# Reordering the tokens of a fused attention + MLP kernel: even tokens first, and transposed queries and keys used straight from the DMA

## The chip, the cores and the metric

The kernel runs on one core of one Trainium2 chip. The metric is the device time of one execution in microseconds (us); three executions of the kernel before took 322.33 to 323.25 us, median 322.83. The profile that is read here is of one execution, with a span of 321.3 us between its first and last instruction.

## The reference, cut to what matters

```python
batch, n_heads, seq, head_dim = (8, 8, 576, 64)          # q, k, v, float32
scores = q @ k.T / 8; mask = abs(pos_q - pos_k) <= 32    # a window of 65 keys per query
attn = softmax(where(mask, scores, -1e9)); a = attn @ v
x = a.transpose(0, 2, 1, 3).reshape(4608, 512)           # 4608 tokens x (8 heads x 64)
h = x @ w_in                                             # w_in 512 x 2048
out = maximum(0.01 * h, h) @ w_out                       # w_out 2048 x 512
```

## The kernel before, in words

**Attention** is cut into 64 instances: batch b (8), half hf of the 576 tokens (2 x 288), pair p of heads (4). Instance i has b = i // 8, hf = (i // 4) % 2, p = i % 4. The two heads of a pair lie on partitions 0 to 63 and 64 to 127. Before, pair p holds heads p and p + 4.

What an instance needs is made as follows. `load_qk` (L73) and `load_v` (L82) bring q, k and v in float32 from DRAM, on the queue of SP. `cast_qk` (L183) turns q and k to bf16 on GpSimd (POOL), on 96 partitions with six tokens each. Then they are transposed, so that head dimension lies on the partitions: for batches 0 to 2 by TensorE (L214, six 96x96 transposes into a PSUM tile `tp` and one ScalarE copy, L222 or L228, into token order); for batches 3 to 7 by a DMA transpose (L200) into a tile of its own, and again one ScalarE copy (L222, L228), SBUF to SBUF, which puts the six residues of the token number back in token order. `place_keys` (L240) copies the transposed keys on VectorE (DVE) into `kbd`, a block-diagonal weight (two copies of 64 partitions x 576 per pair). `cast_v` (L191, or L189 on ScalarE) does the same for v, into `vbd`.

`score` (L255) multiplies five blocks of 64 keys with the queries in their windows, 544 columns in all, into one PSUM tile `ps` of which there is one; ScalarE takes the exponential (L261), POOL multiplies with a 0/1 mask (L265) into `prob`. `join` (L276, from instance 12 on) adds the two halves of `prob` on DVE so that `sums` (L285) needs one matmul of 288 columns; DVE takes the reciprocal (L296). `product` (L307, five matmuls) multiplies with `vbd`, and `scaled` (L322) writes x times the reciprocal into `xT`, the transposed input of the MLP. There is one PSUM buffer for the sums and one for the products.

**The MLP** follows in groups of 288 tokens. `h_tile(g, f)` makes 128 of the 2048 hidden values of a group with four matmuls of 288 columns (L336); `h_out` applies the leaky ReLU on ScalarE from PSUM into `gT` (L342). `o_tile(j)` makes 128 output tokens with 16 matmuls of 512 columns (L373), one ScalarE copy (L378) and one store (L379) on SP. The h and o tiles and the TensorE transposes share a PSUM pool of four buffers.

**The order** on each engine is the program's: `manual_schedule()` keeps it. The first part (batch 0, group 0, batch 1's transposes and group 1's h tiles) is written out by hand. After it a plan of h tiles and quarters of o tiles is walked; `spend` holds a clock in planned us and calls `step()` for the next instance whenever its due time is reached, spread so that the last instance of a group comes `LEAD` = 4 us before the group's first h tile. A `step()` for instance i issues the join of i + 1, the score of i + 2, then sums, product and scaling of i, then whatever transposes, key copies, casts and loads are due. A PLAN table and the counters `state["tp"]` and `asked` say which. Weights `w_in` (8 DMAs) and `w_out` (4) are loaded and cast by DMAs that POOL issues (L465, L471).

Of the kernel before, what the change touches and what calls it, by code (L numbers as in the profile page):

```python
# [16 lines left out]
def kernel(  # L17
# [11 lines left out]

    nc = tc.nc  # L30

    B, H, S, D = q.shape
    W = 32
# [9 lines left out]
    NCOL = 544  # L43
# [10 lines left out]
    tdma = ctx.enter_context(tc.tile_pool(name="tdma", bufs=1))  # L54
# [9 lines left out]

    def load_qk(b, p, behind=None):


        for into, src, name in ((qf, q, "qf"), (kf, k, "kf")):
            t = fload.tile([96, 2, RUN * D], FP32, name=f"{name}{p}")
            if behind is not None:  # L70
                behind.memset(t[0:1, 0, 0:1], 0.0)
                behind = None
            nc.sync.dma_start(  # L73
                out=t, in_=src[b, p:H:NPAIR].rearrange("a (p c) d -> p a (c d)", c=RUN),
            )
            into[b, p] = t

    def load_v(b, p):

        t = fload.tile([128, NB, D], FP32, name=f"vf{p}")  # L80
        for a in range(2):
            nc.sync.dma_start(  # L82
                out=t[64 * a:64 * a + 64],
                in_=v[b, NPAIR * a + p].rearrange("(c p) d -> p c d", p=64),
            )
        vf[b, p] = t
# [29 lines left out]
    def clear(t, p):  # L116
# [4 lines left out]

    nc.vector.memset(kbd[0], 0.0)
# [6 lines left out]

    PAD = 32  # L130
    SPLIT = [HALF - PAD, HALF]
    WIN = [
        [(1, 32, 128), (3, 160, 128), (0, 0, 96), (2, 96, 128), (4, 224, 64)],
        [(4, 288, 64), (6, 352, 128), (8, 480, 96), (5, 288, 128), (7, 416, 128)],
    ]

    win = const.tile([128, 3, 128], BF16)
    nc.gpsimd.memset(win, 1.0)
    for lo in (0, 64):
# [3 lines left out]
            base=0, channel_multiplier=-1, pattern=[[0, 3], [1, 128]],  # L143
# [3 lines left out]
            base=2 * W, channel_multiplier=1, pattern=[[0, 3], [-1, 128]],  # L147
        )
    nc.gpsimd.memset(vbd[0][:, 3], 0.0)
    win_f = win.rearrange("p n c -> p (n c)")  # L150
    mask = [const.tile([128, NCOL], BF16, name=f"mask{i}") for i in range(2)]

    def make_masks():
        for hf in range(2):
            lo = (0, 2 * W)[hf]
            nc.gpsimd.tensor_copy(
                out=mask[hf][:, 0:SPLIT[hf]], in_=win_f[:, lo:lo + SPLIT[hf]],
            )
            lo = (W, 0)[hf]
            nc.gpsimd.tensor_copy(  # L160
                out=mask[hf][:, SPLIT[hf]:NCOL], in_=win_f[:, lo:lo + NCOL - SPLIT[hf]],
            )
    NPROB = 6
    prob = const.tile([128, NPROB, NCOL + 2 * PAD], BF16)
    nc.vector.memset(prob[:, :, 0:PAD], 0.0)
    nc.vector.memset(prob[:, :, PAD + NCOL:], 0.0)

# [9 lines left out]
    def cast_qk(b, p, q_eng=None):  # L177
        for eng, src, dst in ((q_eng or nc.gpsimd, qf, qb), (nc.gpsimd, kf, kb)):
            tok = src[b, p].rearrange("p a (c d) -> p c a d", d=D)
            if eng is nc.scalar:  # L180
                eng.activation(out=dst[:, p], in_=tok, func=AF.Copy)
            else:
                eng.tensor_copy(out=dst[:, p], in_=tok)  # L183
# [9 lines left out]

    BY_DMA = 3
    qkT, asked = {}, {}

    def transpose_dma(b, p):
        for which, src in (("q", qb), ("k", kb)):
            t = tdma.tile([128, RUN, 96], BF16, name=f"{which}T{p}")
            nc.sync.dma_start_transpose(out=t, in_=src[:, p].rearrange("p c a d -> p (c a d)"))  # L200
            qkT[b, p, which] = t
        asked[b, p] = state["done"]

    def transposes(b):

        qT[b] = attn.tile([128, NPAIR, S], BF16, name="qT")
        for p in range(NPAIR):
            for which, src in (("q", qb), ("k", kb)):
                if b >= BY_DMA:
                    tp = qkT.pop((b, p, which))  # L210
                else:
                    tp = mmps.tile([128, RUN, 96], BF16, name="tp", tag="mm")
                for c in range(RUN if b < BY_DMA else 0):
# [6 lines left out]
                tok = tp.rearrange("p c i -> p i c")  # L220
                if which == "q":
                    nc.scalar.activation(  # L222
                        out=qT[b][:, p].rearrange("p (i c) -> p i c", c=RUN), in_=tok, func=AF.Copy,
                    )
                else:
                    kT = kt.tile([128, S], BF16, name="kT")
                    kT_v = kT.rearrange("p (i c) -> p i c", c=RUN)
                    nc.scalar.activation(out=kT_v, in_=tok, func=AF.Copy)  # L228
# [3 lines left out]
    unplaced = []  # L232

    def place_keys():

        while unplaced:
            b, p, kT = unplaced.pop(0)
            for a in range(2):
                r = slice(64 * a, 64 * a + 64)
                nc.vector.tensor_copy(  # L240
                    out=kbd[b % 2][r, p, :, r],
                    in_=kT[r].rearrange("p (n j) -> p n j", j=64),
                )
# [6 lines left out]
    def score(i):  # L250
        b, hf, p = where(i)
        ps = scps.tile([128, 1024], FP32, name="ps")
        lo = c0 = 512 - SPLIT[hf]
        for blk, q0, n in WIN[hf]:
            nc.tensor.matmul(  # L255
                ps[:, c0:c0 + n], kbd[b % 2][:, p, blk],
                qT[b][:, p, q0:q0 + n], start=True, stop=True,
            )
            c0 += n
        e = attn.tile([128, NCOL], BF16, name="e")  # L260
        nc.scalar.activation(  # L261
            out=e, in_=ps[:, lo:lo + NCOL], func=AF.Exp, scale=scale,
        )
        pr = prob[:, i % NPROB, PAD:PAD + NCOL]
        nc.gpsimd.tensor_mul(pr, e, mask[hf])  # L265
        probs[i] = [pr, None, None]
        state["ps"] = ps

    def join(i):


        hf = where(i)[1]
        lo = PAD * hf
        t = prob[:, i % NPROB]
        both = joined.tile([128, HALF], BF16, name="both")
        nc.vector.tensor_add(both, t[:, lo:lo + HALF], t[:, lo + HALF:lo + 2 * HALF])  # L276
        probs[i][1] = both

    def sums(i):
# [6 lines left out]
        else:  # L286
            nc.tensor.matmul(
                s, ones_bd, pr[:, (NCOL - HALF) * (1 - hf):(NCOL - HALF) * (1 - hf) + HALF],
                start=True, stop=False, skip_group_check=True,
            )  # L290
            nc.tensor.matmul(
                s[:, PAD * (1 - hf):PAD * (1 - hf) + NCOL - HALF], ones_bd,
                pr[:, HALF * hf:HALF * hf + NCOL - HALF], start=False, stop=True, skip_group_check=True,
            )
# [4 lines left out]
    def product(i):  # L299
# [4 lines left out]
        c0 = 0  # L304
        for n_, (blk, q0, n) in enumerate(WIN[hf]):
            a = q0 - HALF * hf
            nc.tensor.matmul(  # L307
                x[:, a:a + n], vbd[b % 2][:, p, blk, :], pr[:, c0:c0 + n],
                start=(n_ == 0), stop=(n_ == len(WIN[hf]) - 1), skip_group_check=True,
            )  # L310
            c0 += n
# [29 lines left out]
    def h_out(g, f, h):  # L341
        nc.scalar.activation(  # L342
            out=gT[:, f, ds(g * HALF % RING, HALF)], in_=h[:, 0:HALF], func=AF.Prelu, alpha=0.01,
        )
# [36 lines left out]
    def keep_busy(t, lo, n):  # L381


        for _ in range(n):
            nc.tensor.matmul(
                t[:, lo:lo + 224], ones_bd, mask[0][:, 0:224], start=False, stop=False,
# [6 lines left out]
    state = {"tp": 8, "done": 0}  # L393
    t_parts = {}
# [3 lines left out]

    PLAN = (
        ((0, 0, 0, 0, 0, 2, 4, 6), ((), (), (), (), (0,), (1, 2), (3,), ()),  # L400
         ((), (), (), (), (), (), (0,), (1, 2, 3))),
        ((0, 1, 2, 3, 4, 5, 6, 7), ((0,), (1,), (2,), (3,), (), (), (), ()),
         ((), (), (), (), (0,), (1,), (2,), (3,))),
    )

    def step_transposes(upto):
        while state["tp"] < min(upto, 8 * B):
            b = state["tp"] // 8
            if b not in t_parts:
                t_parts[b] = transposes(b)  # L410
            next(t_parts[b])
            state["tp"] += 1

    def step():
# [3 lines left out]
        b, r = i // 8, i % 8  # L418
        if JOINED - 1 <= i < NC - 1:
            join(i + 1)  # L420
        if b < BY_DMA - 1:
            place_keys()
        if b > 0:
            upto = 8 * (b + 1) + (PLAN[b > 1][0][r] if b + 1 < BY_DMA else 0)
            step_transposes(max(upto - 1, 8 * (b + 1)))
        if 8 <= i < NC - 2:
            nb, _, np_ = where(i + 2)
            if nb >= BY_DMA:
                step_transposes(8 * nb + 2 * np_ + 2)
                if any(key[:2] == (nb, np_) for key in unplaced):  # L430
                    place_keys()
# [3 lines left out]
        if b > 0:  # L435
            step_transposes(upto)
        if 0 < b < B - 1:
            for p in PLAN[b > 1][1][r] if b + 1 <= BY_DMA else ():
                cast_qk(b + 1, p)
                if b + 1 == BY_DMA:  # L440
                    transpose_dma(b + 1, p)
                if b + 2 < B:
                    load_qk(b + 2, p)

            n, p = (b + 1, 3) if r == 0 else (b + 2, r - 4)
            if p in range(4 if r == 0 else 3) and BY_DMA < n < B:
                step_transposes(8 * (n - 1) + 2 * p + 2)
                place_keys()
                cast_qk(n, p)
                transpose_dma(n, p)  # L450
                if n + 1 < B:
                    load_qk(n + 1, p)
            for p in PLAN[b > 1][2][r]:
                cast_v(b + 1, p)
                if b + 2 < B:
                    load_v(b + 2, p)
# [3 lines left out]
    w_in_r = moe_w_in.rearrange("(a u d) f -> a d u f", a=2, d=D)  # L460
# [209 lines left out]
```

The softmax here doesn't subtract the row's maximum and nothing guards it: scores larger than these inputs give would overflow.

## Time and profile before

| | busy us | share of 321.3 us | what it does most |
|---|---|---|---|
| PE (TensorE) | 303.9 | 95% | h tiles 134.3, o tiles 128.6 |
| ACT (ScalarE) | 223.6 | 70% | gT 103.4; the 40 SBUF-to-SBUF copies of L222 and L228 47.2 |
| DVE (VectorE) | 212.7 | 66% | reciprocals 125.1; key copies 28.5 |
| POOL (GpSimd) | 182.3 | 57% | masks 77.8; casts of v, k and q 86.8 |
| PEld (weight load) | 205.9 | 64% | overlaps PE |

An engine's busy time is no limit by itself: the table shows which engine has no room, and that a long ScalarE copy need not cost anything if PE never waits for it. The DMA queues moved 48.28 MB; HBM was read for 36.70 MB.

### The profile page before, as it was taken

To read this page: it belongs to the slowest core of one execution; us is meant where nothing else is said; L and a number is where in the kernel's file an instruction comes from. 1 tells how busy PE (TensorE), PEld (TensorE's weight loads), DVE (VectorE), ACT (ScalarE), POOL (GpSimd) and SP (SyncE) were. 2 spreads that over 40 slices of the span, in tenths; PEclk is the share of its full clock that TensorE was granted. 3 is DMA by queue.
4 is the path that set the end of the run, shared out by engine and by line. 5 is a ranking of instruction groups with operands and counts; after the bars stand their busy time and mean duration, and the time that the engine had idled before them with its cause. 6 is when DMAs were issued, how large, how long until landed. Compare 5 with 4: busy or idle time off the path is not lost.

```text
span 321.3 us, 6563 instructions
## 1 busy us (share of the span) xinstructions
PE 303.9 (95%) x2476; PEld 205.9 (64%) x2497; DVE 212.7 (66%) x259; ACT 223.6 (70%) x432; POOL 182.3 (57%) x215
## 2 busy tenths in 40 slices
PE   2779999999999999999999999999999999999995
PEld 1566775586765857676665857676665857576753
DVE  5788784986757679676748778677747666565100
ACT  7586584296658897888887887888885837464631
POOL 8999967677945976269612885269612653230000
PEclk9999999999999999999999999999999999999999
DMA  8999998999997999929991399728611000000101
GB/s 185 229 176 233 267 236 208 259 224 233 207 192 192 214 242 234 175 73 179 236 221 71 94 216 229 177 65 134 166 39 65 36 34 35 33 36 0 67 33 66
DMA packets 85168, 48.28 MB, mean 150 GB/s; under 512 B 64016, under 2 KB 80656, under 8 KB 85136
## 3 DMA queue, kind: packets, MB, share of 16 engines
q1 hardware_dynamic: 80848, 43.66, 62.8%
q0 software_dynamic: 4288, 4.20, 8.0%
q8 instruction: 19, 0.31, 0.4%
q14 instruction: 13, 0.11, 0.2%
HBM read 36.70 MB, written 9.44 MB: 144 GB/s over the span
## 4 chain that ended last, share of the span: by engine, by line
PE 79%; POOL 6%; DMA 6%; DVE 4%; ACT 3%; issue 2%; POOLq 0%; DVEq 0%; ACTq 0%
PE mm L373 35%; PE mm L336 33%; DMA w_out_bf<-in_moe_w_out_dram 6%; PE x L307 4%; PE ps L255 4%; DVE r L296 2%; PE s L285 2%; POOL prob L265 2%; POOL kb L183 1%; ACT kT L228 1%; DVE xT L322 1%; PE tp L214 1%; POOL w_in_bf L465 1%; ACT e L261 1%; ACT gT L342 0%
## 5 line engine op out<-in xcount | busy, mean ns | idle before, releaser
L296 DVE RECIPROCAL r<-s 128x288 f32<-128x288 f32 x64 | 125.1, 1955 | 56.6 <-PE s L285 53.5
L336 PE MATMUL mm<-xT,w_in_bf 128*128 128x288 bf16 x1024 | 134.3, 286 | 0.9 <-DMA w_in_bf<-in_moe_w_in_dram 0.7
L265 POOL TENSOR_TENSOR prob<-e,mask 128x544 bf16<-128x544 bf16 x64 | 77.8, 1215 | 99.6 <-ACT e L261 79.5
L373 PE MATMUL mm<-w_out_bf,gT 128*128 128x512 bf16 (+2 forms) x571 | 128.6, 373 | 1.6 <-DMA w_out_bf<-in_moe_w_out_dram 0.5
L342 ACT ACTIVATE gT<-mm 128x288 bf16<-128x288 f32 x256 | 103.4, 413 | 24.9 <-PE mm L336 10.0
L336 PEld LDWEIGHTS <-w_in_bf 128*128 128x128 bf16 x1024 | 97.8, 98 | 25.6 <-issue 1.8
L373 PEld LDWEIGHTS <-gT 128*128 128x128 bf16 x592 | 56.0, 98 | 59.9 <-issue 0.6
L378 ACT ACTIVATE o_sb<-mm 128x512 f32<-128x512 f32 (+2 forms) x37 | 21.7, 586 | 53.8 <-PE mm L373 53.8
L261 ACT ACTIVATE e<-ps 128x544 bf16<-128x544 f32 x64 | 39.8, 622 | 9.5 <-PE ps L255 8.8
L191 POOL CAST vbd<-vf 64x576 bf16<-64x576 f32 x58 | 38.5, 663 | 3.7 <-DMA vf<-in_v_dram 1.9
L240 DVE COPY kbd<-kT 64x576 bf16<-64x576 bf16 x64 | 28.5, 445 | 16.3 <-ACT kT L228 15.6
L322 DVE TENSOR_TENSOR xT<-x,r 128x288 bf16<-128x288 f32 x64 | 29.3, 458 | 9.0 <-PE x L307 2.4
L183 POOL CAST kb<-kf 96x768 bf16<-96x768 f32 x32 | 28.6, 895 | 2.6 <-DMA kf<-in_k_dram 2.6
L255 PEld LDWEIGHTS <-kbd 128*128 128x128 bf16 x320 | 21.5, 99 | 10.2 <-DVE kbd L240 1.4
L255 PE MATMUL ps<-qT,kbd 128*128 128x128 bf16 (+2 forms) x320 | 26.3, 214 | 1.7 <-DVE kbd L240 1.2
L307 PE MATMUL x<-prob,vbd 128*128 128x128 bf16 (+2 forms) x320 | 26.0, 213 | 1.1 <-DVE xT L322 1.0
L307 PEld LDWEIGHTS <-vbd 128*128 128x128 bf16 x320 | 21.4, 99 | 3.9 <-DVE xT L322 1.0
L222 ACT ACTIVATE qT<-qT 128x576 bf16<-128x576 bf16 x20 | 23.6, 1182 | 0.0
L228 ACT ACTIVATE kT<-kT 128x576 bf16<-128x576 bf16 x20 | 23.6, 1180 | 0.0
L276 DVE TENSOR_TENSOR both<-prob 128x288 bf16<-128x288 bf16 x52 | 22.8, 438 | 0.6
L183 POOL CAST qb<-qf 96x768 bf16<-96x768 f32 x24 | 19.7, 823 | 0.0
L285 PE MATMUL s<-both,ones_bd 128*128 128x288 bf16 x52 | 14.9, 286 | 0.0
(45 smaller groups left out, 102.0 us busy)
## 6 DMA issues: line engine op xcount, KB each, us to landing
qf<-in_q_dram SPq DMA_DIRECT2D x32, 288.0 KB, 4.2
kf<-in_k_dram SPq DMA_DIRECT2D x32, 288.0 KB, 4.6
vf<-in_v_dram SPq DMA_DIRECT2D x64, 144.0 KB, 4.9
out_dram<-o_sb SPq DMA_DIRECT2D x35, 256.0 KB, 2.8
w_in_bf<-in_moe_w_in_dram POOLq DMA_DIRECT2D x8, 256.0 KB, 7.9
w_out_bf<-in_moe_w_out_dram POOLq DMA_DIRECT2D x4, 512.0 KB, 16.3
qT<-qb SPq DMA_TRANSPOSE x20, 4.0
kT<-kb SPq DMA_TRANSPOSE x20, 3.3
```

The costliest lines, as they stand in the source:

```text
L183: eng.tensor_copy(out=dst[:, p], in_=tok)
L191: nc.gpsimd.tensor_copy(out=vbd[b % 2][r, p, :, r], in_=vf[b, p][r])
L240: nc.vector.tensor_copy(out=kbd[b % 2][r, p, :, r], in_=kT[r].rearrange("p (n j) -> p n j", j=64),)
L255: nc.tensor.matmul(ps[:, c0:c0 + n], kbd[b % 2][:, p, blk], qT[b][:, p, q0:q0 + n], start=True, stop=True,)
L261: nc.scalar.activation(out=e, in_=ps[:, lo:lo + NCOL], func=AF.Exp, scale=scale,)
L265: nc.gpsimd.tensor_mul(pr, e, mask[hf])
L296: nc.vector.reciprocal(r, s)
L307: nc.tensor.matmul(x[:, a:a + n], vbd[b % 2][:, p, blk, :], pr[:, c0:c0 + n], start=(n_ == 0), stop=(n_ == len(WIN[hf]) - 1), skip_group_c ...
L322: nc.vector.tensor_mul(place(i), x, r)
L336: nc.tensor.matmul(h[:, 0:HALF], w_in_bf[:, c, ts(f, 128)], xT[:, c, ds(g * HALF % RING, HALF)], start=(c == 0), stop=(c == DMC - 1),)
L342: nc.scalar.activation(out=gT[:, f, ds(g * HALF % RING, HALF)], in_=h[:, 0:HALF], func=AF.Prelu, alpha=0.01,)
L373: nc.tensor.matmul(o[:, lo:hi], gT[:, f, ds(128 * j % RING, 128)], w_out_bf[:, f, lo:hi], start=(f == 0), stop=(f == FFC - 1),)
```

## The change: what it does

- In every half of 288 tokens, the even tokens come first and then the odd ones, from the queries through `prob`, x and `xT` to the h matmuls. `h_out` undoes it: it reads PSUM with the two parities interleaved and writes `gT` in token order.
- For batches 2 to 7 q and k are loaded in rows of two tokens (512 bytes) instead of six (1536 bytes), and cast in two pieces each, so that the DMA transpose delivers the queries in the even-first order. It writes right into `qT` and `kT`; the ScalarE copies that followed it are gone, and batch 2 is no longer transposed by TensorE. The keys' order is undone in the DVE copy into `kbd`, which then writes with a step of two elements. It is issued two steps after the transpose.
- Batches 0 and 1 keep the TensorE transposes and ScalarE copies; only the order in which the copy of the queries reads PSUM differs.
- Score, mask and `prob` have 576 columns (two layers of 288) instead of 544; matmuls of a block run over two stretches (even, odd) and have the same total of 544 columns. `ps` is one fixed tile.
- Pairs are heads 2p and 2p + 1, so `w_in` is loaded in its natural order, by 4 DMAs of 128 partitions instead of 8 of 64. The loads of `w_in` and `w_out` are issued one place earlier.
- v of batch 1 is cast by ScalarE instead of POOL; the due times of instances 8 to 11 move a little, and the second half's instances go behind h tiles 7, 11, 14 instead of 7, 10, 13. q and k of batch b are cast at steps 8(b-1)+2 to +5 and v at +6 to +9, for all b from 2 on, instead of by the PLAN table.

```diff
-    BY_DMA = 3
+    BY_DMA = 2
 load_qk:
-            nc.sync.dma_start(out=t, in_=src[b, p:H:NPAIR].rearrange("a (p c) d -> p a (c d)", c=RUN))
+            heads = src[b, 2 * p:2 * p + 2]
+            if b < BY_DMA:
+                nc.sync.dma_start(out=t, in_=heads.rearrange("a (p c) d -> p a (c d)", c=RUN))
+            else:
+                nc.sync.dma_start(
+                    out=t.rearrange("p a (g e) -> p a g e", g=3),
+                    in_=heads.rearrange("a (g p c) d -> p a g (c d)", g=3, c=2),
+                )
 cast_qk:
+                by_c = src[b, p].rearrange("p a (g c d) -> c p g a d", g=3, c=2)
+                parts = [(dst[:, p, 3 * c:3 * c + 3], by_c[c]) for c in range(2)]
 transpose_dma:
-            t = tdma.tile([128, RUN, 96], BF16, name=f"{which}T{p}")
-            nc.sync.dma_start_transpose(out=t, in_=src[:, p].rearrange("p c a d -> p (c a d)"))
-            qkT[b, p, which] = t
+        for t, src in ((qT[b][:, p], qb), (kT, kb)):
+            nc.sync.dma_start_transpose(
+                out=t.rearrange("p (c i) -> p c i", c=RUN),
+                in_=src[:, p].rearrange("p c a d -> p (c a d)"),
+            )
+        landing.append((state["done"], b, p, kT))
 place_keys:
+        while landing and landing[0][0] + 2 <= state["done"]:
+            unplaced.append(landing.pop(0)[1:])
...
+                    nc.vector.tensor_copy(
+                        out=to.rearrange("p n (m c) -> p n c m", c=2),
+                        in_=kT[r].rearrange("p (c n m) -> p n c m", c=2, n=NB),
+                    )
 score:
-        nc.scalar.activation(out=e, in_=ps[:, lo:lo + NCOL], func=AF.Exp, scale=scale)
-        nc.gpsimd.tensor_mul(pr, e, mask[hf])
+        nc.scalar.activation(out=e, in_=ps[:, P0:P0 + 2 * HALF], func=AF.Exp, scale=scale)
+        nc.gpsimd.tensor_mul(pr.rearrange("p n c i -> p (n c i)"), e, mask[hf].rearrange("p n c i -> p (n c i)"))
 h_out:
-            out=gT[:, f, ds(g * HALF % RING, HALF)], in_=h[:, 0:HALF], func=AF.Prelu, alpha=0.01,
+            out=gT[:, f, ds(g * HALF % RING, HALF)].rearrange("p (i c) -> p i c", c=2),
+            in_=h[:, 0:HALF].rearrange("p (c i) -> p i c", c=2), func=AF.Prelu, alpha=0.01,
 step:
+    for b in range(2, B):
+        for p in range(NPAIR):
+            qk_due.setdefault(8 * (b - 1) + p + 2, []).append((b, p))
+            v_due.setdefault(8 * (b - 1) + p + 6, []).append((b, p))
...
 load_w_in:
-        for a in range(2):
-            nc.gpsimd.dma_start(out=w_in_bf[64 * a:64 * a + 64, :, f0:f1], in_=w_in_r[a, :, :, f0:f1])
+        nc.gpsimd.dma_start(out=w_in_bf[:, :, f0:f1], in_=w_in_r[:, :, f0:f1])
 before and in the plan:
-        prev = 0.9 * O_US * 4 if i < 12 else at[i // 4 - 1] - LEAD
-        due.append(prev + (at[i // 4] - LEAD + (1.2 if i < 12 else 0) - prev) * (i % 4 + 1) / 4)
+        prev = 0.75 * O_US * 4 if i < 12 else at[i // 4 - 1] - LEAD
+        due.append(prev + (at[i // 4] - LEAD + (1.8 if i < 12 else 0) - prev) * (i % 4 + 1) / 4)
-    cast_v(1, 0)
+    cast_v(1, 0, on_act=True)
-                cast_v(1, i - 7)
+                cast_v(1, i - 7, on_act=True)
```

## The prediction, made before the changed kernel was run

> **What bounds the kernel now.** I read the busy times first, then PE in windows, then who waited for whom, then the chain of work that ended last, then the costs of the operations that the change touches. The table of windows shows PE busy 47.57 of the first 60 us, 79.15 of the next 80, 159.42 of the next 160:
>
> ```profile
> 0.00:60.00 60.00, 47.57 (x435) 33.81 (x439) 44.41 (x52) 39.11 (x75) 51.44 (x68) 1.00 1.08 222
> 60.00:140.00 80.00, 79.15 (x662) 53.48 (x667) 58.93 (x77) 60.41 (x116) 50.05 (x58) 1.00 1.04 208
> 140.00:300.00 160.00, 159.42 (x1261) 107.22 (x1270) 109.38 (x132) 115.47 (x223) 80.79 (x90) 1.00 0.49 108
> ```
>
> So from 60 us on TensorE is the bound and hardly waits; what can be won there is TensorE work itself. Only the first 60 us hold idle PE time (12.4 us, of which 5.6 lie before PE's first instruction). The chain says what ends that part:
>
> ```profile
> 29.51 19.63 DMA w_out_bf<-in_moe_w_out_dram
> 49.14 0.04 issue
> 49.18 2.75 PE mm L373 x12
> ```
>
> The last quarter of `w_out` lands at 49.14 us, and the first o tile waits for it. PE waits before that are paid again at this wait, so shortening them wins nothing unless the weights come earlier. The engine queues in the waits view and the rows of the touched operations:
>
> ```profile
> PE x L307 <- DVE xT L322: 1.0, 4, 0.4
> PE mm L373 <- DMA w_out_bf<-in_moe_w_out_dram: 0.5, 1, 0.5
> ...
> L342 ACT ACTIVATE gT<-mm 128x288 bf16<-128x288 f32 x256 | 103.4, 413 | 24.9 <-PE mm L336 10.0
> L222 ACT ACTIVATE qT<-qT 128x576 bf16<-128x576 bf16 x20 | 23.6, 1182 | 0.0
> L222 ACT ACTIVATE qT<-tp 128x576 bf16<-128x576 bf16 x12 | 7.9, 655 | 4.5 <-PE tp L214 4.5
> L240 DVE COPY kbd<-kT x64: 399/448/451, 7.7 to 244.4; 64x576 bf16<-64x576 bf16 x64
> L183 DVE CAST qb<-qf x7: 630/1262/2258, 4.8 to 45.4; 96x768 bf16<-96x768 f32 x7
> ```
>
> The reader is to see: a ScalarE copy that gathers six residues costs 1182 ns out of SBUF and 655 out of PSUM; the key copy takes the same 448 ns always, while the seven DVE casts take 630 to 2258.
>
> [...] For ScalarE the trace agrees on SBUF (1182) and shows no penalty on PSUM (655 for 576 elements, beside 622 for 544 in a row, L261). [...] the new copy itself is in no run here.
>
> **The change part by part**, against the span of 321.3 us. The three timed runs have a median of 322.83, 1.5 above it; I add 1.5 at the end.
>
> 1. Batch 2's TensorE transposes go: eight groups of six, 0.26 us each in the chain ("PE tp L214 x6"), all on PE between 67 and 84 us where it is the bound: **-2.1 us**.
> 2. 40 ScalarE copies go (47.2 us), and 8 from PSUM. ScalarE isn't the bound: its busy share is 70%. On the path they show only around 107 to 121 us, where the chain runs over qT and kT copies, the key copies behind them, and a reciprocal that is late for it; there PE waits for xT at 121.48 (0.28) and 125.88 (0.20). **-0.5**. A third such wait at 58.32 (0.15) should go with the wider due times of instances 8 to 11: **-0.15**.
> 3. Sums of instances 0 to 11: 576 columns instead of 544, 32/2.4 = 13 ns each, **+0.15**. Scores and products keep their columns. That a matmul's operands come in two stretches no row shows: [...] I take 0[...].
> 4. Exponential and mask: 32 columns more, +0.03 and +0.07 us (622/544 and 1215/544 per column). In the middle both are two steps ahead of their use. Before 25 us they are in a dependent chain, but that ends at the weights' wait: 0.
> 5. `h_out` reads PSUM in alternation. Between 413 (no penalty, as `tp` shows) and 413 + 288 x 0.92 = 680 ns (the SBUF surcharge, (1182-655)/576 per element). I take 413: 0.
> 6. Casts of q and k in halves: v's 576 columns take 665 ns and 768 take 820, so about 185 fixed; +0.19 us a cast, 48 casts, +9 us on POOL. It loses batch 1's v casts (8 x 0.665) and four w_in issues. POOL stays under 60%: 0. SP: the 512-byte rows make 576 pieces a load, as v's 64 x 9 have; v's issue takes 0.63 us against 0.44. A step then needs two transposes (2 x 1.22), two loads and a store, 4.2 us of SP in a step of 4.1 to 4.5. Stores wait behind, four output buffers deep: 0 on PE.
> 7. **The key copies as a new wait on DVE.** A step on DVE is now 0.31 (join) + 1.95 + 0.46 + two copies, 3.79 us from 99.98 to 103.77, thus 2.88 + 2k. Queued behind the copies are the next join, reciprocal and scaling; PE's product waits for the scaling before it, with about 1.2 us of slack, over a step of 4.2. At k = 0.53 (the undisturbed cast's 630 ns for 768 elements; scaled to 576 it is 0.47, with part of it fixed 0.53) nothing is lost; at k = 1.06 (waiting for POOL each time, as the median cast does with twice the shortest) the lag grows by 0.8 a step over four steps of six batches. I take k = 0.8, a wait at every second copy: a lag of 0.84 after three steps, still in the slack, and **+0.4** for steps that fall closer together; bounds 0 and +7. The wait for the landing itself: transposes land 3.3 to 4.0 us after issue, the copy comes two steps (8.4 us) after the cast was issued, whose last piece ends some 4.6 us into its step: covered.
> 8. **v of batch 1 on ScalarE.** POOL waits for these data now; its casts start at 48.09 and 49.62, each "<-DMA vf". ScalarE executes in order: behind its two casts stand the copies of pair 2's transposes (done at 45.2 to 46.5 now), the exponential of instance 9 and pair 3's copies; PE's transposes of pair 3 wait for a PSUM buffer of pair 2's, and score 10 for its keys. Casts end at 49.62+0.68 = 50.3, q's and k's copies at 51.6, key copies at 52.5; score 10 runs at 51.77 now: +0.8. If the buffer decides, transposes wait to 50.95 where 49.18 was: +1.8. If v lands earlier, 0. I take **+0.8**.
> 9. Weights: POOL issues four w_in DMAs (0.79 each, as w_out's equal shape) for eight of 0.66. The DMA share is 1.1 to 1.3 from 5 to 50 us, so the queue is full and an earlier issue moves the end little: 0, with -0.5 (PE's wait) as the other end.
>
> Sum: -2.1 - 0.5 - 0.15 + 0.15 + 0.4 + 0.8 = -1.4; 321.3 - 1.4 = 319.9, and with 1.5 **321.4 us**.
>
> **The rivals.** *Nothing is given back* (chance 0.24): v lands with the weights a little earlier and the key copies don't collide. -2.6 - 0.5 gives 318.2, or 319.7 timed. For it: DVE has 34% idle. *The ScalarE hold is long* (0.12): +1.8 and not +0.8, 322.4, within 0.3%. For it: the four-buffer pool. *Slower: key copies behind POOL* (0.18). They fall 3 us into a step, just where POOL runs four half casts or two v casts. At k = 1.0 the lag grows 0.68 a step; after three steps 2.0, less 1.2 slack, 0.84 on PE a batch, six batches 5.0: 321.3 - 2.6 + 0.8 + 5 = 324.5, timed 326.0. It decides from k = 0.91 on, where 0.3 a batch eat the 1.8 us left. Against it: a late PE gives DVE time too. *h_out at 680 ns* (0.04): ScalarE then needs 16 x 0.68 + 1.2 = 12.1 us in a group whose PE part is 9.1; 3 us in 15 groups, 366 us. The change does what it says as far as the code shows.
>
> **How the numbers follow.** The forecast has 0.42, its own range 320.3 to 322.3. A measurement of this kernel tells 0.3%, 0.97 us, from no change: faster is under 321.9. The forecast is faster with 0.30 and the same with 0.12; the first rival faster; the second 0.08 same and 0.04 slower; the other two slower: 0.54, 0.20, 0.26. The range from 318.3 to 326.5 leaves out the last rival, the worse end of the third and a part of the first that would need a gain before 50 us: about 0.18.
>
> **What would show it.** PE's transposes 96 for 144; no SBUF-sourced ScalarE copy; `gT` at 413 to 430 ns; the key copy's minimum at 0.5 to 0.6 us and its median above (step 7 right)[...]; ScalarE waiting for vf near 48 us and PE's next score near 52.6; PE waits for xT in steps with key copies. I am wrong if PE's matmuls of scores get longer, if `gT` does, or if `w_out` lands more than 1 us away from 49.1.

## The result, and the profile after

| | us, median | lowest to highest | profiled span |
|---|---|---|---|
| before | 322.80 | 322.33 to 323.25 | 321.3 |
| after | 327.86 | 327.30 to 328.53 | 326.0 |

The row of before has a fourth execution beside the three named above. The ratio after to before is 1.0158, with a 95% interval of 1.0133 to 1.0182: the change costs 5 us, where the prediction had a gain of 1.4.

PE by stage, after, in the view of busy times by windows (start and end, length, then busy time and instructions of PE, PEld, DVE, ACT and POOL, then the granted clock, DMA share, GB/s):

```profile
0.00:60.00 60.00, 46.35 (x428) 33.32 (x429) 43.48 (x52) 43.85 (x82) 43.92 (x55) 1.00 1.06 215
60.00:140.00 80.00, 76.04 (x593) 49.74 (x593) 58.02 (x67) 41.38 (x92) 50.79 (x70) 0.98 0.93 181
140.00:300.00 160.00, 160.00 (x1280) 107.54 (x1278) 117.88 (x139) 89.58 (x199) 97.12 (x127) 1.00 0.60 130
```

From 140 us on PE never waits, which is better than before (159.42). The loss is ahead of that. Finer windows put it at two places (the first two lines are of before, the others of after):

```profile
40.00:60.00 20.00, 19.28 (x167) 12.23 (x168) 14.34 (x15) 11.70 (x25) 14.61 (x17) 1.00 1.01 230
60.00:100.00 40.00, 39.79 (x351) 27.43 (x354) 27.55 (x37) 26.39 (x56) 26.12 (x31) 1.00 1.07 217
...
40.00:60.00 20.00, 18.07 (x166) 11.62 (x163) 12.76 (x15) 16.18 (x31) 8.65 (x8) 1.00 0.94 207
60.00:100.00 40.00, 36.04 (x274) 23.29 (x274) 28.06 (x32) 20.18 (x45) 23.88 (x33) 0.96 1.12 205
82.39:85.80 3.41, 3.13 (x13) 1.39 (x13) 2.24 (x5) 0.00 (x0) 1.16 (x2) 0.50 1.22 247
```

Before, PE was busy for 19.28 of the 20 us from 40 on and 39.79 of the 40 us from 60 on. The last line is a surprise: for 3.41 us the granted clock is half. Reckoned from each matmul's start to the next one's, the 4.6 us between the two spans are: work -1.9; idle time +1.1 (40 to 60 us), +4.7 (60 to 100) and -0.5 (later); slow clock +1.5 there, and +0.4 at the start, where matmuls of 224 columns come 187 ns apart until full clock is first recorded (at 17.54 us, in before at 16.37) and 95 from then on; the first 40 us and the tail -0.7.

**The first place** is in the chain of waits, just where w_out's landing stood before (start, length, what):

```profile
31.48 16.82 DMA vf<-in_v_dram
...
48.39 0.59 ACT vbd L204
...
49.80 0.66 ACT qT L234
...
50.50 0.42 PE tp L226 x6
```

The first part of batch 1's v lands at 48.3 us. ScalarE stands at its two casts until then, and only after them copies the queries of pair 2 out of PSUM. The next six transposes wait 1.8 us for that PSUM buffer. w_out isn't waited for any more.

**The second place** is in the waits view, from 60 to 100 us (who waited for whom: total us, times, longest):

```profile
DVE kbd L261 <- DMA kT<-kb: 8.2, 3, 4.6
POOL qb L198 <- DMA qf<-in_q_dram: 3.1, 1, 3.1
PE s L302 <- DVE r L310: 2.3, 2, 2.1
PE ps L276 <- DVE kbd L261: 0.8, 1, 0.8
```

DVE waits three times for a transposed key tile (kT) that hasn't landed. Its reciprocal stands behind the waiting copy, and PE's sums wait for the reciprocal. The timeline of PE shows this (start, length, instructions; in brackets the idle time before and what ended it):

```profile
75.30 3.62 PE L388 MATMUL mm<-w_out_bf,gT 128*128 128x512 bf16 x16
79.71 0.41 PE L276 MATMUL ps<-qT,kbd 128*128 128x96 bf16 x5 [0.80 <-DVE kbd L261]
82.20 0.28 PE L302 MATMUL s<-both,ones_bd 128*128 128x288 bf16 x1 [2.07 <-DVE r L310]
82.77 0.64 PE L321 MATMUL x<-prob,vbd 128*128 128x64 bf16 x5 [0.28 <-DVE xT L335]
83.19 4.92 PE L388 MATMUL mm<-w_out_bf,gT 128*128 128x512 bf16 x16
```

The same 16 matmuls take 3.62 us and, after the gap, 4.92. All three waits for keys are batch 2's. SP's queue tells why the keys land late. The lines below are the timeline of SP: its DMA issues, in order, from the transposes of (2,0) to those of (2,1), where (2,1) is pair 1 of batch 2:

```profile
63.11 1.33 SPq L213 DMA_TRANSPOSE qT<-qb  x1
64.54 1.20 SPq L213 DMA_TRANSPOSE kT<-kb  x1
65.80 0.57 SPq L81 DMA_DIRECT2D qf<-in_q_dram  x1
66.42 0.50 SPq L81 DMA_DIRECT2D kf<-in_k_dram  x1
66.97 2.55 SPq L91 DMA_DIRECT2D vf<-in_v_dram  x2
69.61 0.58 SPq L394 DMA_DIRECT2D out_dram<-o_sb  x1
70.29 0.38 SPq L81 DMA_DIRECT2D qf<-in_q_dram  x1
70.72 0.59 SPq L81 DMA_DIRECT2D kf<-in_k_dram  x1
71.39 1.35 SPq L213 DMA_TRANSPOSE qT<-qb  x1
72.84 1.87 SPq L213 DMA_TRANSPOSE kT<-kb  x1
```

The casts of (2,1) end at 67.1 us, but SP is in a row of batch 3's q and k, batch 2's v (2.55 us for two issues), a store and the last q and k of batch 2. The transposes are issued 4.3 us later, at 71.39, and the keys land in time for DVE to start at 77.38; the copy had its turn at 72.77.

The touched operations, from the table of costly groups (busy us, mean ns | idle before):

```profile
L356 ACT ACTIVATE gT<-mm 128x288 bf16<-128x288 f32 x256 | 103.8, 413 | 25.1 <-PE mm L349 6.7
L261 DVE COPY kbd<-kT 64x576 bf16<-64x576 bf16 x48 | 33.5, 698 | 8.5 <-DMA kT<-kb 8.2
L259 DVE COPY kbd<-kT 64x576 bf16<-64x576 bf16 x16 | 7.1, 443 | 8.7 <-ACT kT L240 8.6
L198 POOL CAST qb<-qf 96x384 bf16<-96x384 f32 x48 | 24.6, 539 | 3.1 <-DMA qf<-in_q_dram 3.1
```

`gT` has its 413 ns as before, the strided key copy takes 698 for 443.

### The profile page after: what moved, and what is told of

It is laid out like the page before. It is cut to its first block, busy times and chain, and to the rows that moved or that the text cites. A ratio compares the mean times of both kernels' runs of the same rounds, so it can differ in the third digit from the quotient of the medians.

```text
span 326.0 us, 6476 instructions
## 1 busy us (share of the span) xinstructions
PE 305.3 (94%) x2449; PEld 204.6 (63%) x2449; DVE 221.8 (68%) x259; ACT 184.4 (57%) x393; POOL 191.8 (59%) x251
## 2 busy tenths in 40 slices
DMA packets 108400, 49.46 MB, mean 152 GB/s; under 512 B 68816, under 2 KB 103888, under 8 KB 108368
## 4 chain that ended last, share of the span: by engine, by line
PE 74%; DMA 13%; DVE 5%; POOL 4%; ACT 1%; issue 1%; SPq 0%; DVEq 0%; POOLq 0%; ACTq 0%
PE mm L388 34%; PE mm L349 30%; DMA vf<-in_v_dram 5%; PE x L321 4%; DMA qf<-in_q_dram 3%; PE ps L276 3%; DVE r L310 3%; DMA kT<-kb 3%; POOL prob L283 2%; DMA kf<-in_k_dram 2%; PE s L302 2%; DVE kbd L261 1%; PE s L305 1%; DVE xT L335 1%; POOL kb L198 1%
## 5 line engine op out<-in xcount | busy, mean ns | idle before, releaser
L283 POOL TENSOR_TENSOR prob<-e,mask 128x576 bf16<-128x576 bf16 x64 | 81.6, 1275 | 93.4 <-issue 45.4
L388 PE MATMUL mm<-w_out_bf,gT 128*128 128x512 bf16 (+2 forms) x592 | 131.7, 376 | 0.0
L281 ACT ACTIVATE e<-ps 128x576 bf16<-128x576 f32 x64 | 41.4, 647 | 11.5 <-PE ps L276 11.3
L261 DVE COPY kbd<-kT 64x576 bf16<-64x576 bf16 x48 | 33.5, 698 | 8.5 <-DMA kT<-kb 8.2
L198 POOL CAST kb<-kf 96x384 bf16<-96x384 f32 (+1 forms) x56 | 34.7, 642 | 3.3 <-DMA kf<-in_k_dram 3.1
L206 POOL CAST vbd<-vf 64x576 bf16<-64x576 f32 x50 | 34.8, 696 | 1.6
L198 POOL CAST qb<-qf 96x384 bf16<-96x384 f32 x48 | 24.6, 539 | 3.1 <-DMA qf<-in_q_dram 3.1
L321 PEld LDWEIGHTS <-vbd 128*128 128x128 bf16 x320 | 20.6, 99 | 7.0 <-DVE xT L335 3.3
L293 DVE TENSOR_TENSOR both<-prob 128x288 bf16<-128x288 bf16 x52 | 19.6, 377 | 0.8
L259 DVE COPY kbd<-kT 64x576 bf16<-64x576 bf16 x16 | 7.1, 443 | 8.7 <-ACT kT L240 8.6
L204 ACT ACTIVATE vbd<-vf 64x576 bf16<-64x576 f32 x14 | 9.5, 681 | 3.0 <-DMA vf<-in_v_dram 2.7
```

Of the source, the lines that this page charges most:

```text
L198: eng.tensor_copy(out=to, in_=tok)
L206: nc.gpsimd.tensor_copy(out=vbd[b % 2][r, p, :, r], in_=vf[b, p][r])
L261: nc.vector.tensor_copy(out=to.rearrange("p n (m c) -> p n c m", c=2), in_=kT[r].rearrange("p (c n m) -> p n c m", c=2, n=NB),)
L281: nc.scalar.activation(out=e, in_=ps[:, P0:P0 + 2 * HALF], func=AF.Exp, scale=scale)
L283: nc.gpsimd.tensor_mul(pr.rearrange("p n c i -> p (n c i)"), e, mask[hf].rearrange("p n c i -> p (n c i)"),)
L321: nc.tensor.matmul(x_v[:, :, i0:i0 + n], vbd[b % 2][:, p, blk, :], pr[:, n_, :, i0:i0 + n], start=(blk == parts[0][1]), stop=(blk == parts ...
```

## The experiments

There are five theories. **A**: SP's in-order queue makes batch 2's transposes late. **B**: the key copies come too few steps behind the transposes. **C**: the strided key copies collide with POOL in every batch. **D**: v on ScalarE holds batch 1's transposes. **E**: the halved clock follows from PE's waits and costs time of its own. Each run changes the changed kernel; the kernel before ran beside each on the same chip, and ratios are to it. The diffs are shortened to the lines that matter.

**Order on the queue (A).** x1 puts eight loads of q, k and then eight of v in front:

```diff
-            if i < 12: load_qk(2, i - 8)
+            if i == 8: [load_qk(2, p) for p in range(NPAIR)]
+            if i == 10: [load_v(2, p) for p in range(NPAIR)]
             step()
-            if 10 <= i < 14: load_v(2, i - 10)
```

> The changed kernel, with all four loads of q and k of batch 2 issued at instance 8 and the four of v at instance 10 before its step, ahead of batch 2's first DMA transpose on SP's queue (they came one pair at a time, behind it). Theory A, that SP's queue delays batch 2: the casts of q and k on POOL stop waiting for their data (6.2 us to under 0.5), batch 2's transposes are issued earlier, PE's lost time between 60 and 100 us falls from 6.4 to under 2.5, time about 323 to 324. Theory B, that the key copies are placed too early for the transposes whatever the queue: DVE still waits about 8 us for kT, time above 326. Theory C, that the key copies' contention with POOL costs the time: no change, 327.5 to 328.5.

327.79, ratio 1.0146 (1.0126 to 1.0165): no gain. POOL's wait for the queries went, but the eight issues of v held SP from 61.32 to 68.35 us, ahead of the transposes of (2,0), which were issued at 68.45 for 63.11; DVE then waited 10.1 us for keys. The forecast of 323 to 324 was missed, and the miss says where to look: not at when the loads are asked for, but at what stands ahead of a transpose. x7 has only the first of these lines, and leaves v where it was:

> Batch 2's eight loads of queries and keys all at step 8, its v loads where the changed kernel has them. Theory A: POOL's wait of 3.1 us for the queries of (2,3) goes, and the load issued at 70.3 us is no longer ahead of the transposes of (2,1), which are issued some 1 us earlier; kT waits 5 to 7 us, 326.0 to 327.3. If only the whole stretch of SP's work counts and not its order, nothing moves: 327.5 to 328.2.

325.40, ratio 1.0092 (1.0062 to 1.0123), better than expected: transposes of (2,1) at 69.82 for 71.39, waits for keys 5.9 us. The clock isn't halved in four of the six executions; the other two, with a granted clock of 0.995 and 0.990 in the mean, took 326.36 and 328.35 us. x6 takes batch 3's loads out of the stretch instead:

```diff
-            if b + 1 < B: load_qk(b + 1, p)
+            if 2 < b < B - 1: load_qk(b + 1, p)
+        if 14 <= i < 18: load_qk(3, i - 14)
```

> The loads of batch 3's queries and keys are issued at steps 14 to 17 instead of 10 to 13, where they stand on SP's queue between the transposes and the v loads of batch 2. Theory A (SP's in-order queue makes batch 2 late): each pair of transposes from (2,1) on is issued 1 to 2 us earlier, DVE's waits for kT fall from 8.2 us to 3 to 6, PE's idle time from 60 to 100 us from 4.9 us to 2 to 4, and the time to 325.0 to 326.8, the lower end if the halved clock at 82 us goes too. Theory B (the copies are placed too few steps after their transposes, whatever stands on the queue): kT waits stay at 7 to 9, 327.5 to 328.2.

324.12, ratio 1.0039 (1.0025 to 1.0053), below the expected range. PE waits no longer from 60 to 100 us, but it does after 100:

```profile
60.00:100.00 40.00, 39.72 (x316) 26.08 (x314) 28.68 (x36) 21.76 (x48) 26.20 (x37) 1.00 0.98 197
100.00:140.00 40.00, 37.99 (x296) 24.88 (x295) 30.31 (x35) 20.27 (x45) 26.23 (x36) 1.00 0.95 175
```

The moved loads now stand ahead of the transposes of (3,0), whose first issue took 3.88 us at 98.53: batch 3 inherits a part. A is confirmed, and what counts is what is queued ahead of a transpose.

**Placing of the copies (B).** x2 waits three steps in all batches, x16 in batch 2 alone:

```diff
-        while landing and landing[0][0] + 2 <= state["done"]:
+        while landing and landing[0][0] + 3 <= state["done"]:                                   # x2
+        while landing and landing[0][0] + (3 if landing[0][1] == 2 else 2) <= state["done"]:    # x16
```

> The changed kernel, with the key copies issued three steps after their transposes instead of two. Theory B: DVE's waits for kT (8.2 us) fall under 2, and the loss between 60 and 100 us from 6.4 to 2 to 3, the rest being POOL's late masks; time 323.5 to 325. Theory A: the masks stay late because POOL still waits for q and k of pair 3, and DVE then waits on later pairs; time above 326. Theory C: no change.

> The changed kernel with the key copies three steps after the transposes, for batch 2 alone. Theory B (placed too few steps behind, the rest in order): the waits of TensorE from 60 to 100 us fall as in x2, and those that x2 had after 100 us don't come: 1.5 us below x2's 326.8, at 324.8 to 325.8. Theory A alone (SP's queue): the landing is later than any step that can be waited for, and score waits for the keys instead: 326.5 to 327.9.

x2: 326.83, ratio 1.0110 (1.0090 to 1.0129). Waits for kT fall to 3.0 us, but the score now waits for key copies in later batches too (0.38 us at 123.39, 0.22 at 127.81, and again at 196, 201, 269 and 274). x16: 324.03, ratio 1.0036 (1.0024 to 1.0047), better than either theory had it. Without touching the queue, one step more takes 3.8 us off. What is left is in two places, at 79.92 and 86.45 us, where PE's score waits 0.53 and 1.32 us for the keys. So A and B aren't rivals: the landing is late because of the queue, and it costs this much because DVE waits for it with the reciprocal behind.

**v on ScalarE (D).** x3 gives batch 1's v back to POOL:

```diff
-    cast_v(1, 0, on_act=True)
+    cast_v(1, 0)
-                cast_v(1, i - 7, on_act=True)
+                cast_v(1, i - 7)
```

> The changed kernel, with v of batch 1 cast on POOL as before the change. If ScalarE, which waits for v, holds PE at 48.4 us (1.95 us lost there): PE's loss at that place falls to about 0.6, that of the wait for w_out, and the time by 1.0 to 1.5, to about 326.6. If what is won there is lost behind it (POOL waiting for v in place of ScalarE): 327.5 to 328.5.

325.57, ratio 1.0080 (1.0060 to 1.0101): 2.3 us less than after, more than expected. PE is busy for 19.68 of the 20 us from 40 on, and the halved clock is gone in five of six executions though batch 2 still waits; without that side effect the same edit is worth 1.3 to 1.8 (324.12 to 322.83 from x6 to x10; 324.25 to 322.48 from x9 to x12, below).

**Contention (C).** x4 copies the keys of batches 2 to 7 contiguously, in the order in which the transpose left them, and leaves out their reordering:

```diff
-                        out=to.rearrange("p n (m c) -> p n c m", c=2),
-                        in_=kT[r].rearrange("p (c n m) -> p n c m", c=2, n=NB),
+                        out=to, in_=kT[r].rearrange("p (n j) -> p n j", j=64),
```

> The changed kernel, with the key copies of batches 2 to 7 written in the order in which they lie (step 1), so that the keys in a block stand even first and the scores there are of other keys than the masks suppose. Theory C, contention of the copy with POOL: the copy falls from 698 to about 445 ns and the time by 2 us or more. Theories A and B: the copy is as short, and the time stays within 1 us of 327.9.

326.04, ratio 1.0097 (1.0079 to 1.0115). The copies take 442 ns, yet DVE waits 9.1 us for keys and PE is busy for only 35.74 of the 40 us from 60 on. It gains 1.8 us, and its clock isn't halved in five of six executions, so a cost of C by itself isn't shown here; x12 and x14 below decide it. The collision itself is in the trace of after: every strided copy that begins while POOL is at a cast or a mask ends 0.36 to 0.40 us after that instruction's end. At 77.38 us a mask had 1.07 us to run, that copy took 1.45 us, and the pair 2.27 for the 1.19 of the pair at 68.64, so C made the hold of (2,1) some 1.1 us longer.

**Batch 2 by TensorE again.** x9 undoes that part, with natural loads and contiguous key copies for batch 2:

```diff
-    BY_DMA = 2
+    BY_DMA = 3
+    third = transposes(2)
+        if 12 <= i < 16: next(third); next(third)
-            transpose_dma(b, p)
+            if b >= BY_DMA: transpose_dma(b, p)
```

> Undoes one part: batch 2's queries and keys are loaded in natural order, transposed by TensorE and copied by ScalarE at steps 12 to 15, and its keys copied contiguously; batches 3 on as in the changed kernel. Theory A with B (the loss between 60 and 100 us is batch 2's DMA transposes landing late): idle time there falls from 4.9 us to under 1, the halved clock goes (1.5 us), and 48 transposes cost 2.1 us more: 323.8 to 325.0. Theory C (DVE's slow key copies against POOL are at fault, in every batch): 326.5 to 328.

324.25, ratio 1.0050 (1.0031 to 1.0068): as A with B has it. No wait for kT is left, although batches 3 to 7 still copy with a stride.

**The halved clock (E).** x8 puts 20 dummy matmuls, x13 12, into PE's gap at step 15; they write PSUM columns that nothing reads.

```diff
             score(i + 2)
+        if i == 15:
+            keep_busy(ps, 0, 20)     # x13: 12
```

> Twenty dummy matmuls of 224 columns (some 1.9 us) between the score and the sums of step 15, where TensorE waits 2.24 us for the reciprocal. Theory E (the clock is halved at 82.25 us because TensorE stood idle before it): the halving goes, the granted clock is 0.999 or more, and the time falls by about 1.5 us to 326.1 to 326.7 although there is more work. Rival (the halving has another cause, or only adds to the wait): clock stays at 0.995, 327.7 to 328.3.

> As x8, with 12 dummy matmuls (1.1 us) in place of 20, so that the sums behind them aren't held up. Theory E: no halved clock, and the 1.5 us that it cost come back: 326.1 to 326.7. Rival (the dummies only put their own work in place of the slow clock): 327.3 to 328.0.

x8: 327.31, ratio 1.0133 (1.0112 to 1.0154); x13: 327.10, ratio 1.0131 (1.0112 to 1.0149). In both the halving is gone, in all nine executions. That PE's idle time brings it on is shown. The 1.5 us don't come back: the medians fall by 0.5 to 0.8, and the intervals overlap that of after. The timeline of x13 says where the rest went:

```profile
86.72 0.77 PE L349 MATMUL mm<-xT,w_in_bf 128*128 128x288 bf16 x5 [0.69 <-DVE xT L335]
93.63 0.28 PE L302 MATMUL s<-both,ones_bd 128*128 128x288 bf16 x1 [0.88 <-DVE r L310]
```

After has only 0.23 us of such a wait (at 94.58), and none near 87. My reading is that the next key tiles come when SP issues them, not when PE is ready, and that a slow PE had spent part of that wait at work. By this test E is worth 0.5 to 0.8, not 1.5. The size stays open, for x3, x4, x7, x9 and x10 each had one execution at a mean clock of 0.995, which took 0.8 to 1.7 us longer than the median of the same kernel's executions without it; whether it waited longer too isn't on record.

**Do the losses add up?** x12 is x9 with x3: both losing parts undone, the even-first layout and the strided copies kept. x10 is x6 with x3.

> Both parts that lost are undone: batch 2 by TensorE, batch 1's v on GpSimd; all else is the changed kernel (even tokens first, head pairs, qT used as it lands, strided key copies). If these two account for the whole loss: 322.3 to 323.2, the kernel before within 0.5 us. If the even-first layout itself costs something in every batch (theory C), 323.8 or more.

> Two parts together: batch 1's v on GpSimd as before the change, and batch 3's loads of queries and keys at steps 14 to 17. If the two losses are separate (ScalarE held at 48 us for v; SP's queue at 60 to 100 us), they add: the first is worth 1.0 to 1.5 us without the halved clock, so from 324.1 to 322.6 to 323.3. If removing the first only lets the second grow, 323.8 to 324.5.

x12: 322.48, ratio 0.9986 (0.9978 to 0.9993). x10: 322.83, ratio 0.9992 (0.9973 to 1.0010); two of its 14 executions took 319.97 and 320.61, and why isn't known. In x12 the key copies of batches 3 to 7 take 690 ns in the median, and PE never waits from 100 to 300 us:

```profile
100.00:140.00 40.00, 40.00 (x324) 26.85 (x322) 31.28 (x36) 22.38 (x51) 27.83 (x38) 1.00 0.83 180
140.00:300.00 160.00, 160.00 (x1272) 107.23 (x1270) 115.99 (x138) 88.39 (x197) 93.01 (x122) 1.00 0.60 124
```

So C costs nothing where the keys have landed in time. D and A with B are the whole loss. They add up in x10 as well.

**A version that beats both.** x11 is x3 and x7, with v of batch 2 spread over steps 9 (two), 11 and 12, and batch 3's q and k at steps 13 to 16. x14 moves the v loads behind the first transposes; x15 also copies the keys of (2,0) a step later.

```diff
-            if 10 <= i < 14: load_v(2, i - 10)
+            for p in {9: (0, 1), 11: (2,), 12: (3,)}.get(i, ()): load_v(2, p)    # x11
+            for p in {11: (0,), 12: (1,), 13: (2, 3)}.get(i, ()): load_v(2, p)   # x14, x15
+        if 13 <= i < 17: load_qk(3, i - 13)
```

> A version that should beat both: batch 1's v on GpSimd; all of batch 2's queries and keys loaded at step 8; its v at the end of steps 9 (two), 11 and 12, where SP's queue is empty; batch 3's queries and keys at steps 13 to 16, one step earlier than in x10, so that they don't stand ahead of the transposes of (3,0). Theory A: no wait for a key tile over 1 us from 60 to 140 us, TensorE idle there under 1 us in all, 320.5 to 322.3. If SP's or the DMA engines' work as such is too much for this stretch in whatever order, a wait of 1.5 us or more stays in 60 to 140 us: 322.5 to 324.0.

322.98, ratio 1.0000 (0.9990 to 1.0010), short of the hope: the v loads of step 9 held SP from 60.16 to 64.0 us, the transposes of (2,0) came at 64.09 behind them, and DVE waited 2.9 us for that one tile.

> x11 with batch 2's v loads at the end of steps 11, 12 and 13 (two), so that none stands ahead of the transposes of (2,0), which x11 issued at 64.1 us behind 3.8 us of v loads. If the order on SP's queue is the whole cause of the one wait left in x11 (2.9 us for the key tile of (2,0), 2.4 us of TensorE's idle time), it goes: TensorE idle from 60 to 100 us at most 1.5 us, 320.6 to 322.0. If the DMA engines have too much to do there in whatever order, another key tile is waited for in its place: 322.5 to 323.5.

> x14 with the copies of the keys of (2,0) one step later, since steps 11 and 12 last 3.0 and 3.5 us where later ones last over 4. If those short steps are what is left of theory B: no wait for a key tile over 0.5 us, 320.4 to 321.8, below x14 by 0.2 or more if x14 still waits. If two pairs of copies in one step (2.3 us of VectorE) hold the reciprocal instead: 322 to 323.

x14: **320.46**, ratio 0.9916 (0.9899 to 0.9932). x15: 320.21, ratio 0.9921 (0.9897 to 0.9945), the same, so the extra step is no longer needed once the queue is in order. x14's SP queue, from the transposes of (2,0) on, and its windows:

```profile
61.06 1.32 SPq L213 DMA_TRANSPOSE qT<-qb  x1
62.48 1.21 SPq L213 DMA_TRANSPOSE kT<-kb  x1
63.78 0.54 SPq L394 DMA_DIRECT2D out_dram<-o_sb  x1
64.42 1.25 SPq L213 DMA_TRANSPOSE qT<-qb  x1
65.76 1.99 SPq L213 DMA_TRANSPOSE kT<-kb  x1
67.80 1.31 SPq L91 DMA_DIRECT2D vf<-in_v_dram  x2
```

```profile
40.00:60.00 20.00, 19.83 (x174) 12.30 (x171) 14.91 (x16) 12.12 (x25) 15.07 (x18) 1.00 1.14 229
60.00:100.00 40.00, 39.72 (x314) 26.07 (x313) 29.79 (x35) 21.12 (x46) 26.81 (x38) 1.00 1.05 199
```

Between the transposes of (2,0) and (2,1) there is now one store, where after had seven issues. DVE's waits for kT are 1.1 us in all for 8.2, and that one wait is batch 3's. The bytes are the same (49.46 MB) and the DMA share from 60 to 100 us is 1.05 for 1.12. x11 and x14 differ in nothing but the place of the v loads, and in 2.5 us: it was the order, not the amount. What wasn't tried is a second queue for the v loads.

## Why the prediction was wrong, step by step

- **Step 1** (-2.1) was right in mechanism and size. x12 and x14 differ in where batch 2 is transposed and in the order of the loads that this needs; their ratios, 0.9986 and 0.9916, are 0.7% apart, some 2.3 us. In the changed kernel itself the gain was there (96 transposes for 144) and was lost in waits.
- **Step 2** was right: ScalarE's busy time falls from 223.6 to 184.4 us, and the PE waits for xT at 121 and 126 us are gone. The third, of 0.15 us at 58.32, stayed (0.14 at 59.92).
- **Steps 3, 4 and 5** were right: a score matmul of 128 columns takes 223 ns for 222, the exponential 647 for 622, the mask 1275 for 1215, `gT` 413. The 2.4 columns a ns in step 3's sum is what the traces show: matmuls of 512 columns start 216 ns apart and those of 288 columns 122, which is 2.37 and 2.36. The 0 that step 3 took for operands in two stretches was the author's estimate. That the even and odd stretches and the interleaved PSUM read cost nothing is what lets x12 and x14 work.
- **Step 6** was right on POOL's share (59% busy), though two half casts of q take 1.08 us for 0.82, so 0.26 more and not 0.19; it was wrong on SP. "4.2 us of SP in a step of 4.1 to 4.5" counts a step of a later batch. In batch 2's own steps v is loaded too, and the last q and k of the batch itself: from 63.11 to 71.39 us SP is busy for 7.7 us, in steps that began at 62.74, 65.19 and 69.68. "Stores wait behind" named the wrong victim; the transposes waited.
- **Step 7 failed in its last sentence**: "The wait for the landing itself: [...] covered." Its first half, the cast, held (67.1 us, 4.4 into the step that began at 62.74). But it let the issue follow the cast at once: 4.3 us lay between. And it took 3.3 to 4.0 us to the landing, where (2,1) took 4.5 from the issue of its kT. Even its own figures left little over: 4.6 and 3.3 to 4.0 make 7.9 to 8.6 of 8.4 us, without the issue of kT behind that of qT (1.22 by its step 6); what it had in reserve is that a copy comes some 3 us into its step. From batch 3 on this is enough, and no copy in after waits: for (4,1) the casts end at 144.2 us, the keys land at 147.46 and the copy starts at 150.72. In batch 2 the two steps last 6.9 us for 8.4, and the queue takes 4.3. The copy that was covered by 8.4 us waited 4.62, and everything behind it on DVE with it. x16 (one step more) takes 3.8 us away, and in x14 (nothing ahead but a store) DVE doesn't wait for any key tile of batch 2. The contention part of step 7 was priced well: k of 0.70 (shortest 0.50) for 0.8. The rival built on it, key copies behind POOL, came nearest to the measured time, but by luck, for its reason was wrong: x12 has the same copies and no loss. That a DVE instruction can stand behind POOL, on which its k of 1.06 rested, shows in the trace of before: all seven DVE casts end 0.41 to 0.42 us after the end of a POOL instruction that they overlap, and the shortest (0.63 us, at 6.76), which it called undisturbed, is one of them.
- **Step 8** took +0.8 and the bound named for the buffer, +1.8, is what came: the transposes wait 1.8 us, and the next score runs at 53.34 us where the sum had 52.6. x10 and x12 give 1.3 and 1.8 for it. The mechanism was right; the choice between the two ends wasn't reasoned, though the pool of four buffers had been named.
- **Step 9**: the wait for w_out of 0.46 us went, as its better end had it, and the wait for v took its place at the same point. w_out landed at 48.06 us for 49.14, so the earlier issue did move it, by a little more than the 1 us that the prediction had named as a sign of being wrong.
- **The clock** was in no step. Taken away by itself (x8, x13) it gives 0.5 to 0.8 back.

So from -1.4 to +5 are 6.4 us: in the profile's account about 1 from step 8, and 4.7 of waits and 1.5 of slow clock from the landing that was called covered, less 0.7 at the start and the end.

## What to carry to other kernels

When a transfer takes over work from an engine, write out its queue for the first batch that uses it, issue by issue, not only for the steady state: start-up loads, the next batch's loads and stores stand ahead of it in order (in after the transposes of (2,1) stood behind seven issues and went out 4.3 us after the end of their casts). Place loads that have time behind transfers that have none, and if a copy must wait for a landing, see what stands behind that copy on its engine. A wait that looks covered by a few us in the steady state is to be checked against the shortest steps.

## What the runs showed of the hardware

- **A granted clock of half followed steps of 3.41 us in which PE was idle for 2.07 us or more.** The stretches of full and half clock that the traces of before and after record are whole numbers of 3.413 us long, unless the trace's end cuts them: in before 303.79 us (89 times that) and then a cut one, in after 64.85 us (19), 3.41 us (the half clock) and a cut one. The windows of these steps, with PE's busy time first (the step before the clock halved in after; the one in x1, where it was half from 78.54 to 81.95 us; one step of x3; two of x7):

```profile
78.98:82.39 3.41, 0.60 (x6) 0.30 (x6) 3.27 (x4) 1.22 (x2) 2.45 (x4) 1.00 1.31 204
...
75.13:78.54 3.41, 1.34 (x16) 0.84 (x14) 2.45 (x3) 0.65 (x1) 2.27 (x3) 1.00 1.14 247
...
78.37:81.78 3.41, 1.62 (x12) 0.75 (x12) 2.29 (x3) 0.18 (x1) 2.54 (x3) 1.00 1.21 229
...
81.03:84.44 3.41, 2.25 (x12) 1.07 (x11) 3.37 (x4) 0.60 (x1) 1.32 (x2) 1.00 1.19 217
84.44:87.86 3.42, 2.26 (x25) 1.91 (x25) 1.41 (x3) 1.72 (x4) 0.37 (x1) 1.00 0.99 115
```

PE was idle for 2.81 us of the first of these steps and 2.07 of the second, and the next step ran at half clock. x3 has the same longest wait as after, 2.07 us, and x7 one of 2.32, but a boundary cut them: these steps of theirs have 1.79, 1.16 and 1.16 us idle, and the clock stayed full. Among all recorded steps of before and after that another step follows, the two with the most idle time (2.81 us at 78.98 in after, 2.32 us at 316.74 in before) were followed by half clock, and the third (1.87 us at 321.33 in after) was not. So in these runs it was neither the longest wait nor the sum of a row of waits that told, but what fell into one step; by this reading it is in part luck that x3, x4 and x7 mostly kept their clock. PE need not have been idle for the whole step: it ran matmuls for 0.60 us of the one in after and for 1.34 us of the one in x1.

- **A strided key copy ended after the POOL instruction that was running.** In after, 45 of the 48 began while POOL was at a cast or a mask, took 0.50 to 1.45 us with what POOL had left to do, and ended 0.36 to 0.40 us after that instruction; the two that met no POOL work took 0.51 and 0.52 us. The contiguous copies took 0.39 to 0.45 us in before and after, and 52 of these 80 met POOL work.
- **An issue on SP took longer behind a run of loads.** Two v issues take 1.30 us in quiet stretches and 2.55 at 66.97; eight in a row took 7.03 (x1); the first transpose behind a run of loads took 2.67 (x1) and 3.88 (x6), where most take 1.2 to 1.4.
